# Delta attention, token mixing and two MLPs on one core: the mix's token sum turned, its values split in two

## The chip, the cores and the metric

One core of a Trainium2 chip runs the whole program in a single launch. The metric is the device time in microseconds (us), the median over runs of the same program; smaller is better. The engines are called by their short names: PE (TensorE matmuls, with PEld for its weight loads), DVE (VectorE), ACT (ScalarE), POOL (GpSimd) and SP (the queue that issues most DMAs). Each engine works through its own instructions in the order in which they stand in the program, so an instruction that waits holds up all that stand behind it on that engine.

## The reference

Three stages follow each other on arrays of 4 batches, 768 tokens and 8 heads of 48 (384 columns in all):

```python
# 1 attention, token by token, for each batch and head
y[t] = q[t] @ state
state += beta[t] * outer(k_n[t], v[t] - k_n[t] @ state)
# 2 x is y with heads side by side: mix over the tokens, then an MLP
u = x + (x.transpose(0, 2, 1) @ U @ V).transpose(0, 2, 1)   # U: 768 x 32, V: 32 x 768
x = u + relu(u @ w_ch1) @ w_ch2                              # 384 -> 1536 -> 384
# 3 Fourier mixing, normalisation, a second MLP
u = x + real(fft(fft(x, axis=1), axis=2))
x = u + relu(normalised(u) @ w2_ch1) @ w2_ch2
```

The weights and U and V come as 64-bit floats, q, k, v and beta as 32-bit floats.

## The kernel before, in words

**Stages and tiles.** The attention works on 24 units (chunks) of 128 tokens, six to a batch, numbered 0 to 23. What a unit needs from its keys and queries alone is prepared ahead: scales and 16-bit high and low parts (`s_front`), transposed copies by DMA (`s_turn`), the masked products G (`s_prep_a`, line 841) and their split into a high part `GPh` and a low part `GPl` (`s_split`; the low part is mostly a POOL subtraction, recorded at the helper's line 251), and a triangular inverse `Nf` (`s_prep_b`, `s_prep_c`). Then `s_solve` treats the units one after the other, since each needs the state `S` that the one before left: three small products with `Nf`, corrections, an update of the state and, last, the output `vt` (line 1142, ACT).

**The mix.** `mix_chunk` (line 1010) takes each finished unit. It stores `vt` to DRAM (`xnd`), and multiplies it with the 128 rows of U that belong to it: three fp32 matmuls with `vt` as weights and U as 32 moving columns (line 1026), into `ps_hu`, 128 x 96. DVE adds that to the batch's sum `hu` (lines 1030, 1032). When a batch's six units are in, `s_mix` turns the sum with three PE transposes (line 1283), makes a high and a low part of it (`hst`, lines 1286 and 1288), and multiplies those with three row groups of V (`Vst`: high, high and low part) in fp32r matmuls of 384 columns (line 1305), 128 tokens at a time. DVE adds the tokens' own values (line 1307); scales, splits and a transposing DMA give the input `u` of the first MLP.

**The MLPs.** `s_mlp` handles 8 tiles of 384 tokens in 12 steps each, for both MLPs. A step is nine matmuls into `ps_h` (line 1190), a ReLU on ACT that writes `hh` (line 1196), the low part `hl` on DVE (line 1209; in the attention stage at times PE and ACT, lines 1204 and 1206), and nine matmuls into the accumulators (line 1226), one step behind. `ps_h` of the first MLP has a single PSUM buffer. `s_out1` adds the result, stores it to `x1d` and sums squares.

**The Fourier stage.** It reuses memory that the attention gave up. For each batch, `fold` loads rows of `x1d` forward (SP) and mirrored (indirect DMA on POOL) into `xq`, forms sums and differences `pm` (POOL, line 251), and splits them into `fs` (ACT, line 1451; DVE, line 1453); two rounds of matmuls follow (lines 1485 and 1507). The second MLP's weights are loaded and squared at the same time (`weight2_streams`, lines 483 to 496).

**What sets the order.** No hardware scheduler does. While the program is built, the class `Weave` runs a list scheduler over some twenty generators ("streams"): each says what it wants next, on which engines it may run and for how many modelled nanoseconds; the request with the smallest start time plus its stream's bias is emitted. Biases and prices stand in tables at the top of the file (`PR0`, `PR`, `P2`, `PRICE0` and others), one set until batch 0 is mixed, one until the attention ends, one behind it. `UP` is the number of units whose small sums are made on PE instead of DVE, `UE` the number whose `GPl` is made on PE and ACT instead of POOL.

The two places of the old mix that the change rewrites:

```python
for k in range(KD):                                    # mix_chunk, line 1026
    nc.tensor.matmul(ps[:, k, :], xf[:, 128 * k:128 * k + 128], self.UU[:, c, :], start=True, stop=True)
for k in range(KD):                                    # s_mix, line 1283
    nc.tensor.transpose(ps[0:32, 128 * k:128 * k + 128], hu[:, k, :], self.id32)
```

Of the kernel before, what the change touches and what calls it, by code (L numbers as in the profile page):

```python
# [34 lines left out]
AGE0 = -5  # L35
AGE = 16
EPS0 = -1085
FILL = 47
EPS = -309
UP = 13  # L40
UE = 0
# [3 lines left out]
SPARE = 270  # L45
SPW = 120
PR0 = (-337, -112, -95, -78, -360, -173, -425, 225)
PR = (-41, -98, -140, -142, 118, 51, -956, -408)
ME = -78
MX = -401  # L50
MB = -515
MB0 = -564
P2 = (-467, -323, -887, -360, -372, -386, -1140, -392)
MP = 39
HB = -550
WB1 = -575
WB = -15
PRICE0 = {'p': 1.0, 'v': 1.45, 'a': 0.71, 'g': 0.38}
PRICE = {'p': 1.0, 'v': 0.29, 'a': 0.22, 'g': 0.14}
PRICE2 = {'p': 1.0, 'v': 283.18, 'a': 3.3, 'g': 1.14}  # L60
# [137 lines left out]
def _v(n, rate=1):  # L198
    return 67 + n / (0.96 * rate)
# [14 lines left out]
class Builder:  # L214
# [39 lines left out]
    def setup(self):  # L254
# [23 lines left out]
        self.Vst = c.tile([96, S], F32R, name="Vst")  # L278
# [39 lines left out]
    def mix_parts(self):  # L318

        nc = self.nc  # L320
        self.UU = self.cst.tile([128, NC, 32], F32, name="UU")
        n = NC * 32

        def conv_u(raw, done):
# [3 lines left out]
            nc.scalar.activation(out=self.UU, in_=f, func=ACTF.Copy)  # L328
            self.wv.post("U")

        def conv_v(j):
            def conv(raw, done):
                f = yield from self.from_f64(raw[0:96], self.f64_tile()[0:96])
# [406 lines left out]
    def s_turn(self):  # L740

        nc = self.nc
        for u, _ in self.each():
# [4 lines left out]
            KT = un["KT"] = self.ap1.tile([128, 2, H, 128], F16, tag="KT", name="KT", bufs=NK)  # L748
# [261 lines left out]
    def mix_chunk(self, u):  # L1010
# [5 lines left out]
        if c == 0 and b >= 2:  # L1016
            yield ("hst", b - 2)
# [735 lines left out]
```

## Time and profile before

| what | value |
|---|---|
| median of 3 runs | 1037.67 us (1035.9 to 1040.18) |
| the profiled execution | 1041.91 us, its span 1039.8 us |
| PE busy | 913.1 us, 88% of the span |
| DVE busy | 724.9 us, 70% |
| ACT busy | 548.6 us, 53% |
| POOL busy | 352.2 us, 34% |
| mean granted PE clock | 0.939 of full speed |

The span is the time from the first to the last instruction; the profiled execution's own time is 2.1 us longer. It is one execution, 4.2 us above the median of the runs. An engine's busy share is a mean over three stages: the attention of batch 0 (to about 208 us), the other batches' attention woven with the first MLP (to about 577 us), and the rest of the first MLP, the Fourier stage and the second MLP.

### The profile page before, as it was taken

How to read it: one execution, taken by the hardware profiler on the slowest of the kernel's cores; microseconds unless marked ns; L12 is line 12 of the kernel's file. 1: busy time of each engine (PE TensorE's matmuls, PEld its weight loads, DVE VectorE, ACT ScalarE, POOL GpSimd, SP SyncE). 2: the span in 40 equal slices, each digit the busy share in tenths (PEclk: the TensorE clock that was granted, in tenths of full speed). 3: DMA queues.
4: the chain of work that ended last, by engine and by line, in shares of the span. 5: the costliest groups of instructions: out<-in, count | busy, mean ns of one | idle time of the engine just before them, and what ended most of it. 6: DMA issues, size and time to landing. Idle time of an engine off the chain costs nothing. (4 is left out here: it accounts for less than half of the span.)

```text
span 1039.8 us, 25511 instructions
## 1 busy us (share of the span) xinstructions
PE 913.1 (88%) x10282; PEld 622.6 (60%) x10282; DVE 724.9 (70%) x1664; ACT 548.6 (53%) x1358; POOL 352.2 (34%) x330
## 2 busy tenths in 40 slices
PE   3465777589999899999999879999999999999998
PEld 2344665356777666676676546655756665655655
DVE  6898889898898998998765367765735554444532
ACT  5665676767777766667655244447723232222221
POOL 3554244213444323454110360046555532012010
PEclk8575989589999999999999989999999999999999
DMA  6996677316756565543502546522211311202110
GB/s 189 224 219 163 160 183 174 78 39 146 152 133 162 105 151 112 142 109 79 114 25 70 164 105 192 130 87 71 35 54 50 95 28 54 69 24 61 58 34 23
DMA packets 158253, 110.87 MB, mean 107 GB/s; under 512 B 117484, under 2 KB 146424, under 8 KB 158136
## 3 DMA queue, kind: packets, MB, share of 16 engines
q1 hardware_dynamic: 155688, 102.01, 40.6%
q0 software_dynamic: 2448, 7.24, 2.5%
q8 instruction: 80, 1.31, 0.5%
q14 instruction: 37, 0.30, 0.1%
HBM read 55.63 MB, written 14.16 MB: 67 GB/s over the span
## 5 line engine op out<-in xcount | busy, mean ns | idle before, releaser
L1226 PE MATMUL acc<-w2s,hh 128*128 128x384 f16 x1152 | 281.8, 326 | 4.9 <-DVE u L1624 3.1
L1190 PEld LDWEIGHTS <-w1s 128*128 128x128 f16 x1728 | 163.5, 98 | 114.5 <-issue 14.7
L1196 ACT ACTIVATE hh<-ps_h 128x384 f16<-128x384 f32 x192 | 93.7, 488 | 205.6 <-PE ps_h L1190 201.8
L251 POOL TENSOR_TENSOR GPl<-g,GPh 128x512 f16<-128x512 f32 x92 | 116.1, 1262 | 235.1 <-ACT GPh L244 174.2
L1209 DVE SCALAR_TENSOR_TENSOR hl<-ps_h,hh 128x384 f16<-128x384 f32 x147 | 81.6, 555 | 161.6 <-ACT hh L1196 155.8
L1226 PE MATMUL acc<-w2s,hl 128*128 128x384 f16 x576 | 188.1, 327 | 0.2 <-DVE hl L1209 0.2
L1190 PE MATMUL ps_h<-u,w1s 128*128 128x384 f16 x864 | 169.6, 329 | 11.9 <-DVE hl L1209 10.5
L1190 PE MATMUL ps_h<-uh,w1s 128*128 128x384 f16 x864 | 157.9, 327 | 0.0
L1226 PEld LDWEIGHTS <-hh 128*128 128x128 f16 x1152 | 106.2, 98 | 64.8 <-issue 8.0
L902 PEld LDWEIGHTS <-bd 128*128 128x128 f16 x1728 | 71.6, 99 | 45.7 <-issue 18.6
L1226 PEld LDWEIGHTS <-hl 128*128 128x128 f16 x576 | 56.2, 98 | 38.2 <-DVE hl L1209 0.6
L841 DVE TENSOR_TENSOR g<-ps_g,mask 128x512 f32<-128x512 f32 x96 | 65.6, 683 | 12.1 <-PE ps_g L835 11.0
L834 PE MATMUL ps_g<-KT,BT 128*128 128x256 f16 x192 | 54.0, 301 | 10.0 <-ACT t L993 5.0
L244 ACT ACTIVATE GPh<-g 128x512 f16<-128x512 f32 x75 | 47.0, 626 | 28.0 <-DVE g L841 27.3
L251 POOL TENSOR_TENSOR pair<-x1f,pair 128x384 f16<-128x384 f32 x24 | 22.2, 925 | 111.8 <-ACT pair L1594 106.8
L251 POOL TENSOR_TENSOR pm<-xq 97x768 f32<-97x768 f32 (+1 forms) x16 | 29.3, 1850 | 79.5 <-DMA xq<-x1d 72.1
L835 PE MATMUL ps_g<-K,BT 128*128 128x256 f16 x192 | 54.6, 305 | 1.9 <-DMA K<-KT 1.8
L1068 ACT ACTIVATE rh<-res 128x384 f16<-128x384 f32 x63 | 30.5, 484 | 20.0 <-PE res L1055 10.2
L902 PE MATMUL lanes<-R,bd 128*128 128x32 f16 x768 | 34.7, 179 | 4.5 <-ACT R L244 2.9
L882 DVE TENSOR_TENSOR bd<-Xc,mmask 128x1024 f16<-128x1024 f16 x48 | 34.2, 712 | 5.9 <-ACT Xc L936 5.5
L1055 PEld LDWEIGHTS <-GPh 128*128 128x128 f16 x768 | 30.2, 98 | 9.7 <-issue 6.7
L251 POOL TENSOR_TENSOR kb<-kq,rb 128x384 f32<-128x384 f32 x21 | 18.2, 867 | 50.8 <-DVE rb L658 10.9
(270 smaller groups left out, 1866.6 us busy)
## 6 DMA issues: line engine op xcount, KB each, us to landing
wst<-in_moe_w_ch_dram SPq DMA_DIRECT2D x51, 384.0 KB, 3.4
K<-KT SPq DMA_DIRECT2D x46, 256.0 KB, 3.9
kq<-in_k_dram SPq DMA_DIRECT2D x24, 192.0 KB, 3.8
kq<-in_q_dram SPq DMA_DIRECT2D x24, 192.0 KB, 4.2
vt<-in_v_dram SPq DMA_DIRECT2D x24, 192.0 KB, 2.9
xnd<-vt SPq DMA_DIRECT2D x24, 192.0 KB, 3.5
xn<-xnd SPq DMA_DIRECT2D x24, 192.0 KB, 3.0
x1d<-u SPq DMA_DIRECT2D x24, 192.0 KB, 1.9
```

The lines of the kernel that those rows point to most:

```text
L244: self.nc.scalar.activation(out=out, in_=in_, func=ACTF.Copy)
L251: (self.nc.vector if eng == "v" else self.nc.gpsimd).tensor_tensor(out=out, in0=in0, in1=in1, op=op)
L834: nc.tensor.matmul(o, BT[:, h, :], KT[:, :, h, :], start=i == 0, stop=False, skip_group_check=True)
L835: nc.tensor.matmul(o, BT[:, h, :], K2[:, :, h, :], start=False, stop=True, skip_group_check=True)
L841: nc.vector.tensor_tensor(out=g32.rearrange("p i (a t) -> p (i a) t", a=2), in0=ps.rearrange("p i (a t) -> p (i a) t", a=2), in1=self.mask ...
L882: self.nc.vector.tensor_tensor(out=dst.rearrange("p h (j c) -> p h j c", j=n), in0=x, in1=mask[:, None, :, :].to_broadcast(shape), op=ALU. ...
L902: nc.tensor.matmul(ps[:, h, :], lhs[:, h, :], rhs[:, h, :], start=plus is None, stop=plus is None or h == H - 1)
L1068: nc.scalar.activation(out=t, in_=R, func=ACTF.Copy, scale=-1.0 / SC)
L1190: nc.tensor.matmul(ps[:, i, :], w[:, k, fs], u[x][:, k, :], start=(m == 0), stop=(m == 3 * KD - 1))
L1196: nc.scalar.activation(out=hh, in_=ps, func=ACTF.Relu, scale=1.0 if wi else 1.0 - 2.0 ** -11)
L1209: nc.vector.scalar_tensor_tensor(out=hl, in0=ps, scalar=0.0, in1=hh, op0=ALU.max, op1=ALU.subtract)
L1226: nc.tensor.matmul(acc, h[:, ds_], w, start=(f == 0 and j == 0), stop=(f == KF - 1 and j == 2))
```

## The change

The sum over tokens is now formed turned. U is the stationary operand: `UU` holds its high and its low fp32r part, 64 columns, and the unit's values stream past it. The values are split first: ACT writes the high part `yh` of `vt`, POOL or DVE the rest `yl` (also recorded under the name `yh`). Two fp32r matmuls of 384 columns then give `ps_hu` (64 x 384): both parts of U with `yh`, and U's high part with `yl`. DVE adds all 384 columns into `SH`, a single tile that holds the mix's sum in its lower 64 partitions and the attention's state, moved from `S32`, in its upper 64. At a batch's end there is nothing to transpose: ACT and DVE write the four row groups of `hst` from `SH`, and `Vst` has a fourth group. `KT` has five buffers, not six. All numbers that set the order are new, `UP` is 11 for 13 and `UE` 4 for 0.

```diff
-AGE0 = -5
+AGE0 = 6
...
-UP = 13
-UE = 0
+UP = 11
+UE = 4
...
-PR0 = (-337, -112, -95, -78, -360, -173, -425, 225)
+PR0 = (-219, -196, -172, -118, -335, -164, 311, 58)
...
-        self.Vst = c.tile([96, S], F32R, name="Vst")
+        self.Vst = c.tile([128, S], F32R, name="Vst")
+        self.SH = self.keep.tile([128, H, D], F32, name="SH")
...
-        self.UU = self.cst.tile([128, NC, 32], F32, name="UU")
+        self.UU = self.cst.tile([128, NC, 64], F32R, name="UU")
...
-            nc.scalar.activation(out=self.UU, in_=f, func=ACTF.Copy)
+            nc.scalar.activation(out=self.UU[:, :, 0:32], in_=f, func=ACTF.Copy)
+            yield {"w": _v(n)}
+            nc.vector.tensor_tensor(out=self.UU[:, :, 32:64], in0=f, in1=self.UU[:, :, 0:32].bitcast(F32), op=ALU.subtract)
...
-            KT = un["KT"] = self.ap1.tile([128, 2, H, 128], F16, tag="KT", name="KT", bufs=NK)
+            KT = un["KT"] = self.ap1.tile([128, 2, H, 128], F16, tag="KT", name="KT", bufs=NF + 1)
...
-        if c == 0 and b >= 2:
-            yield ("hst", b - 2)
+        if c == 0 and b >= 1:
+            yield ("hst", b - 1)
...
+        yh, yl = (self.ap1.tile([128, DM], F32R, tag=f"y{x}", name="yh", bufs=1) for x in "hl")
+        yield {"a": _a(DM)}
+        nc.scalar.activation(out=yh, in_=xf, func=ACTF.Copy)
+        e = yield {"w": _v(DM), "g": _g(DM)}
+        self.tt(e, yl, xf, yh.bitcast(F32), ALU.subtract)
         t = yield from self.take()
-        ps = self.psu.tile([128, KD, 32], F32, tag="psu", name="ps_hu")
-        yield {"p": 680 if self.wv.warm else 1280}
-        for k in range(KD):
-            nc.tensor.matmul(ps[:, k, :], xf[:, 128 * k:128 * k + 128], self.UU[:, c, :], start=True, stop=True)
-        yield {"v": _v(32 * KD)}
+        ps = self.psu.tile([128, DM], F32, tag="psu", name="ps_hu")
+        yield {"p": 380 if self.wv.warm else 660}
+        nc.tensor.matmul(ps[0:64], self.UU[:, c, :], yh, start=True, stop=False, skip_group_check=True)
+        nc.tensor.matmul(ps[0:32], self.UU[:, c, 0:32], yl, start=False, stop=True, skip_group_check=True)
+        yield {"v": _v(DM)}
+        hu = self.SH[0:64].rearrange("p h d -> p (h d)")
...
-            nc.vector.tensor_tensor(out=self.hu[b], in0=self.hu[b], in1=ps, op=ALU.add)
+            nc.vector.tensor_tensor(out=hu, in0=hu, in1=ps[0:64], op=ALU.add)
...
-                t, ps = yield from self.mix_bank(n, 0)
-                yield {"p": 330}
-                for k in range(KD):
-                    nc.tensor.transpose(ps[0:32, 128 * k:128 * k + 128], hu[:, k, :], self.id32)
...
+                nc.scalar.activation(out=hst[64:128], in_=hu[0:64], func=ACTF.Copy)
...
+                nc.scalar.activation(out=hst[0:32], in_=hu[0:32], func=ACTF.Copy)
...
+                nc.vector.tensor_tensor(out=hst[32:64], in0=hu[0:32], in1=hst[0:32].bitcast(F32), op=ALU.subtract)
```

Since the numbers are new, the whole order moves. Line numbers of the changed kernel are a few higher for the same statements (1142 is 1150, 1196 is 1204, 1451 is 1455). Three places follow.

**ACT around the first MLP's first step.** `hh` is the step's ReLU, `rh`, `U` and `d` are parts of unit 6's solve, `w1s` and `w2s` are splits of the first MLP's weights. Before:

```order
L244 ACTIVATE GPh<-g_3468 128x512
L365 ACTIVATE w2s<-wf_1794,few 128x384
L936 ACTIVATE Xc<-lanes 128x256
L365 ACTIVATE w1s<-wf_2198,few 128x384
L244 ACTIVATE d_3616<-ps_s 128x384
L365 ACTIVATE w1s<-wf_2198,few 128x384
L244 ACTIVATE R<-lanes 128x256
L365 ACTIVATE w1s<-wf_2198,few 128x384
L244 ACTIVATE R<-lanes 128x256
L1196 ACTIVATE hh<-ps_h 128x384
```

With the change:

```order
L244 ACTIVATE t_142<-Zs 32x8x32
L373 ACTIVATE wf_1544<-wf_1544,few 128x384
L368 ACTIVATE w2s<-wf_1544,few 128x384
L996 ACTIVATE t_144<-ps_x 64x512
L244 ACTIVATE Sst<-SH 64x384
L368 ACTIVATE w2s<-wf_1544,few 128x384
L1150 ACTIVATE vt<-ps_s,dn 128x384
L244 ACTIVATE nf_136<-ps_n 64x8x64
L368 ACTIVATE w1s<-wf_1988,few 128x384
L1027 ACTIVATE yh<-vt 128x384
L1204 ACTIVATE hh<-ps_h 128x384
```

Before, the first `hh` stood behind one of unit 6's three `rh`; now it stands behind all three, the unit's output `vt` and its `yh`. Of the 24 weight splits on ACT (lines 365 and 368), 21 stood ahead of the first `hh`, now 13.

**ACT at the end of the attention.** `vt` is unit 23's output, `fs` the first split of the Fourier stage. Before:

```order
L1142 ACTIVATE vt<-ps_s,dn 128x384
L1286 ACTIVATE hst<-ps_u 32x384 x2
L1196 ACTIVATE hh<-ps_h 128x384 x2
L496 ACTIVATE wst,wsq<-wf_11642 128x384
L1196 ACTIVATE hh<-ps_h 128x384 x2
L496 ACTIVATE wst,wsq<-wf_11642 128x384
L1196 ACTIVATE hh<-ps_h 128x384
L1451 ACTIVATE fs<-pm,few 97x4x193
```

With the change; unit 23's `vt` is the row just ahead of the first one here:

```order
L1027 ACTIVATE yh<-vt 128x384
L1321 ACTIVATE xn<-u_11341,few 128x384
L1204 ACTIVATE hh<-ps_h 128x384 x3
L499 ACTIVATE wst,wsq<-wf_11659 128x384
L1204 ACTIVATE hh<-ps_h 128x384
L499 ACTIVATE wst,wsq<-wf_11659 128x384
L1204 ACTIVATE hh<-ps_h 128x384 x3
L499 ACTIVATE wst,wsq<-wf_11659 128x384
L1204 ACTIVATE hh<-ps_h 128x384
L1289 ACTIVATE hst<-SH 64x384
L1291 ACTIVATE hst<-SH 32x384
L1455 ACTIVATE fs<-pm,few 97x4x193
```

Between the last `vt` and the first `fs` stood five `hh`; now there are eight. On DVE, five `hl` stood between the last sum of the mix and the first `fs`, now seven.

**POOL near the end of the attention.** `GPl` is the low part of G, four to a unit; `yh` is the new subtraction `yl`. Before:

```order
L251 TENSOR_TENSOR kb<-kq,rb 128x384
L251 TENSOR_TENSOR kq<-kq,n_r_9661 128x384
L251 TENSOR_TENSOR GPl<-g_9758,GPh 128x512
L251 TENSOR_TENSOR kb_127<-kb,kb_127 128x8x48
L251 TENSOR_TENSOR kq_119<-kq,kq_119 128x8x48
L251 TENSOR_TENSOR GPl<-g_9891,GPh 128x512
L251 TENSOR_TENSOR GPl<-g_9960,GPh 128x512
L251 TENSOR_TENSOR GPl<-g_9999,GPh 128x512
L251 TENSOR_TENSOR GPl<-g_10351,GPh 128x512
L251 TENSOR_TENSOR GPl<-g_10456,GPh 128x512
L251 TENSOR_TENSOR GPl<-g_10525,GPh 128x512
```

With the change:

```order
L251 TENSOR_TENSOR yh<-vt,yh 128x384
L251 TENSOR_TENSOR kb<-kq,rb 128x384
L251 TENSOR_TENSOR kq<-kq,n_r_9744 128x384
L251 TENSOR_TENSOR GPl<-g_9723,GPh 128x512
L251 TENSOR_TENSOR kb_128<-kb,kb_128 128x8x48
L251 TENSOR_TENSOR kq_120<-kq,kq_120 128x8x48
L251 TENSOR_TENSOR GPl<-g_9825,GPh 128x512
L251 TENSOR_TENSOR GPl<-g_9983,GPh 128x512
L251 TENSOR_TENSOR yh<-vt,yh 128x384
L251 TENSOR_TENSOR GPl<-g_10135,GPh 128x512
L251 TENSOR_TENSOR GPl<-g_10242,GPh 128x512
```

POOL had nothing that depended on a solve; now 24 such subtractions stand among the `GPl`. Each stands behind the `GPl` of at least one whole later unit, where there is one. The number of `GPl` on POOL falls from 92 to 77.

## Rows read from the trace of the kernel before

**Rows 1.** The page, section 1: the span.

```profile
span 1039.8 us, 25511 instructions
```

**Rows 2.** Windows: length, five engines' busy time (instructions), PE clock, DMA, GB/s.

```profile
0.00:208.00 208.00, 122.13 (x1970) 93.96 (x1971) 175.27 (x403) 135.97 (x335) 88.51 (x94) 0.74 0.72 174
208.00:577.00 369.00, 350.26 (x5471) 255.20 (x5470) 308.65 (x683) 250.62 (x630) 115.21 (x99) 0.99 0.49 109
577.00:1040.00 463.00, 440.70 (x2843) 273.48 (x2842) 240.98 (x579) 161.99 (x394) 148.44 (x137) 0.99 0.27 74
```

**Rows 3.** Timeline of PE, 268 to 300 us: start, length, what, count.

```profile
274.93 0.36 PE L1055 MATMUL ps_s<-Ul,GPh 128*128 128x48 f16 x8
275.13 0.48 PE L1226 MATMUL acc<-w2s,hh 128*128 128x384 f16 x2
...
281.80 0.85 PE L1026 MATMUL ps_hu<-UU,vt 128*128 128x32 f32 x6
282.49 0.36 PE L1055 MATMUL ps_s<-rh,nf 128*128 128x48 f16 x8
```

**Rows 4.** Timeline of PE, 346 to 349.5 us.

```profile
347.04 0.44 PE L1305 MATMUL ps_u<-hst,Vst 96*128 96x384 f32 x1 [1.37 <-DVE g L841]
347.32 0.37 PE L902 MATMUL lanes<-Nc,bd 128*128 128x32 f16 x8
```

**Rows 5.** Timeline of PE, 463 to 466.5 us.

```profile
465.86 0.50 PE L1283 MATMUL ps_u<-id,hu 128*32 128x128 f32 x3 [1.00 <-DVE g L841]
```

**Rows 6.** By line and form: count | busy us, mean ns | idle before.

```profile
L251 POOL TENSOR_TENSOR GPl<-g,GPh 128x512 f16<-128x512 f32 x92 | 116.1, 1262 | 235.1 <-ACT GPh L244 174.2 <-DVE GPh L246 25.5 <-PE ps_hu L1026 11.6
...
L251 POOL TENSOR_TENSOR pair<-x1f,pair 128x384 f16<-128x384 f32 x24 | 22.2, 925 | 111.8 <-ACT pair L1594 106.8 <-ACT a L1491 5.0
...
L1142 ACT ACTIVATE vt<-ps_s,dn 128x384 f32<-128x384 f32 x24 | 13.8, 576 | 9.8 <-PE ps_s L1055 9.6
...
L1307 DVE TENSOR_TENSOR u<-ps_u,xn 128x384 f32<-128x384 f32 x24 | 13.3, 556 | 5.9 <-PE ps_u L1305 5.7
...
L1594 ACT ACTIVATE pair<-x1f 128x384 f16<-128x384 f32 x24 | 12.5, 521 | 17.5 <-DVE x1f L1591 17.5
...
L1032 DVE TENSOR_TENSOR hu<-hu,ps_hu 128x96 f32<-128x96 f32 x20 | 5.0, 248 | 7.6 <-PE ps_hu L1026 7.5
```

**Rows 7.** Timeline of ACT, 570 to 606 us [idle before <-releaser].

```profile
574.21 0.58 ACT L1142 ACTIVATE vt<-ps_s,dn 128x384 f32<-128x384 f32 x1 [0.52 <-PE ps_s L1055]
...
591.04 0.49 ACT L1196 ACTIVATE hh<-ps_h 128x384 f16<-128x384 f32 x1 [1.99 <-PE ps_h L1190]
600.49 0.94 ACT L1451 ACTIVATE fs<-pm,few 97x772 f16<-97x772 f32 x1 [8.96 <-POOL pm L251]
```

**Rows 8.** Timeline of POOL, 560 to 625 us.

```profile
577.40 1.37 POOL L1405 MEMSET xq<- 1x1536 f32 x1 [50.28 <-PE ps_hu L1026]
...
592.50 3.71 POOL L251 TENSOR_TENSOR pm<-xq 97x768 f32<-97x768 f32 x2 [6.71 <-DMA xq<-x1d]
```

**Rows 9.** Waits of PE, 577 to 1040 us: total, times, longest.

```profile
PE ps_h L1190 <- DVE hl L1209: 9.5, 3, 8.1
```

**Rows 10.** Chain that ended last: start us, us, what.

```profile
603.48 3.04 PE ps_h L1190 x9
606.51 1.93 PE acc L1226 x9
608.44 1.46 PE ps_h L1190 x9
```

**Rows 11.** Timeline of DVE, 20 to 60 us.

```profile
29.61 1.63 DVE L882 TENSOR_TENSOR bd<-GPh,mmask 128x1024 f16<-128x1024 f16 x1
...
39.42 0.69 DVE L882 TENSOR_TENSOR bd<-Xc,mmask 128x1024 f16<-128x1024 f16 x1
```

**Rows 12.** Timeline of POOL, 28 to 41 us.

```profile
29.23 1.47 POOL L251 TENSOR_TENSOR GPl<-g,GPh 128x512 f16<-128x512 f32 x1
...
37.95 0.91 POOL L251 TENSOR_TENSOR kq<-kq,kq 128x384 f16<-128x384 f32 x1
```

More of the change, by code (lines that the diff above doesn't have):

```diff
@@ L44 @@
 UA = 8
-SPARE = 270
-SPW = 120
-PR0 = (-337, -112, -95, -78, -360, -173, -425, 225)
[L48 to L60, printed above, removed]
+SPARE = 288
+SPW = 98
+PR0 = (-219, -196, -172, -118, -335, -164, 311, 58)
+PR = (-150, -119, -395, -76, 118, -67, -532, -601)
+ME = -102
+MX = -503
+MB = -536
+MB0 = -501
+P2 = (-481, -124, -812, -369, -388, -404, -1582, -255)
+MP = 1
+HB = -662
+WB1 = -218
+WB = -4
+PRICE0 = {'p': 1.0, 'v': 1.74, 'a': 0.42, 'g': 0.24}
+PRICE = {'p': 1.0, 'v': 0.44, 'a': 0.51, 'g': 0.2}
+PRICE2 = {'p': 1.0, 'v': 2028.58, 'a': 0.78, 'g': 0.22}
 SC = 16.0
@@ L347, in mix_parts @@
             src = self.words(self.V[:, HALF * j:HALF * j + HALF])
-            parts.append(([(lambda raw, i=i: raw[32 * i:32 * i + 32], src, 273) for i in range(3)], conv_v(j)))
+            parts.append(([(lambda raw, i=i: raw[32 * i:32 * i + 32], src, 273) for i in range(4)], conv_v(j)))
         return parts
@@ L1049, in f16t, with hmm @@
             return self.ap1.tile([128, H, D], F16, tag=tag, name=tag)
-        def hmm(ps, terms, whole=(), m=128, mode="chain", start=True, stop=True):
+        def hmm(ps, terms, whole=(), m=128, mode="chain", start=True, stop=True, at=0):
             yield {"r" if whole else "p": self.pe(len(terms) * H, 48, m)["p"] + self.pe(len(whole), DM)["p"]}, mode
@@ L1054, in hmm @@
                 for h in range(H):
-                    nc.tensor.matmul(ps[0:m, h, :], lf(h), x[:, h, :], start=start and i == 0 and h == 0,
+                    nc.tensor.matmul(ps[at:at + m, h, :], lf(h), x[:, h, :], start=start and i == 0 and h == 0,
                                      stop=stop and not whole and i == len(terms) - 1 and h == H - 1, skip_group_check=ps is R)
@@ L1139, in s_solve @@
                 St = self.ap2.tile([128, H, D], F16, tag="Sst", name="Sst")
-                yield from self.cp(St[0:64], S32, n, "chain")
+                yield from self.cp(St[64:128], S32, n, "chain")
             yield {"a": _a(n, True) + 94}, "side"
@@ L1277, in s_mix @@
                     self.wv.warm = True
[L1278 to L1290 removed]
+                hu = self.SH.rearrange("p h d -> p (h d)")
+                hst = self.keep.tile([128, DM], F32R, tag="hst", name="hst")
+                yield {"a": _a(DM)}
+                nc.scalar.activation(out=hst[64:128], in_=hu[0:64], func=ACTF.Copy)
+                yield {"a": _a(DM)}, "par"
+                nc.scalar.activation(out=hst[0:32], in_=hu[0:32], func=ACTF.Copy)
+                yield {"v": _v(DM)}, "par"
+                nc.vector.tensor_tensor(out=hst[32:64], in0=hu[0:32], in1=hst[0:32].bitcast(F32), op=ALU.subtract)
+                yield "join"
                 self.wv.post("hst", b)
```

32 lines of the change are left out of this document (11 added, 21 removed).

## The prediction

> **What bounds the kernel now.** I read the span first [rows 1], then the busy times in three stretches [rows 2], and after that only places where PE stands still.
>
> The first stretch, 208 us, is the attention of batch 0. PE is busy for 122 us, DVE for 175 (84%). Preparing a unit and solving it pass through many small DVE and ACT steps there; a little PE work more or less is not what ends this stretch.
>
> The second, 369 us, weaves the other 18 units with the first MLP. PE is busy 350 us (95%) at 0.99 of the 2.4 GHz level, DVE 309 (84%), ACT 251, POOL 115. Work taken off PE shortens this stretch, provided that DVE and the chain of solves keep up.
>
> The third, 463 us, is PE too: 441 us busy, 22 idle. More than a third of that idle time is one wait of 8.1 us, of `ps_h` for DVE's `hl` [rows 9]. The reader can follow its cause: POOL starts to clear `xq` at 577.40, when the attention has freed the memory, and reaches the first `pm` at 592.50, after 6.71 us of waiting for rows of `x1d` [rows 8]. ACT has `fs` next in its order, so it stands idle for 8.96 us and starts it at 600.49, and the sixth `hh` stands behind it [rows 7]. `ps_h` has one buffer, so PE stops. Then nine matmuls take 3.04 us and the next nine 1.93, against 1.46 for the same count after that [rows 10]: 2.1 us more, lost to a start at half speed.
>
> **The change, part by part.** The sum is made against the profiled execution, 1041.9 us; the median of the runs is 4.2 us below it, and I take that off at the end. About 0.5%, 5.2 us, is what a measurement of this kernel can tell from no change.
>
> *The mix's matmuls.* Before, a unit's six records start at 281.80 and the next work at 282.49: 0.69 us of PE [rows 3]. Now there are two fp32r matmuls of 384 columns. The nearest row is `ps_u`, of that kind and width, which starts at 347.04 and is followed at 347.32: 0.28 us [rows 4], so 0.56 for two. The gain is 0.13 x 18 units = 2.3 us in the second stretch. Bounds: 0.44 each if the recorded length counted in full (3.4 us lost), 0.16 each if they ran like fp16 (1.46 / 9, [rows 10]; 6.7 us gained). I take 2.3, since type and width are those of `ps_u`. In the first stretch the six units count for nothing: PE idles there for 86 us.
>
> *The transposes.* Three records of 0.50 us a batch go away [rows 5], for three batches in the second stretch: 1.0 to 1.5 us; I take 1.0, since the last record's tail overlaps with what follows.
>
> *Work moved ahead of the first MLP.* By the order, PE now does unit 6's solve ahead of the first `ps_h`. Counted in matmuls behind the first `ps_h`, there are 13 groups of eight small ones fewer (0.20 us each, [rows 3]), 24 single ones for the state (0.03, an estimate between 0.20 / 8 and 0.36 / 8 of those rows), 16 of 256 columns and 4 of 384 (0.11 and 0.16, from 1.46 / 9): 2.6 + 0.7 + 1.8 + 0.6 = 5.7 us. That is a gain only if the first `ps_h` comes no later, which is the next term.
>
> *The first stretch.* Added on DVE: six evacuations of 384 columns for 96, 0.556 for 0.248 [rows 6], 1.8 us, and one split of U, some 0.3. ACT gets 6 x 0.52 for `yh`, and 16 copies of `GPl` at about 0.58 (the row of `vt`, from PSUM, is nearest), 12 us on 136. POOL loses 16 x 1.26 us of `GPl` and gets six subtractions of 0.93 (as `pair`). Against that, 355 DVE instructions now stand ahead of batch 0's low part of `hst`, where 366 stood: 11 x 0.435 (175.27 / 403), 4.8 us less. But the first `hh` now stands behind the whole of unit 6's solve on ACT, and each unit's mix comes 0.52 + 0.93 us later. I take 0, with -5 and +9 (six times 1.45) as ends.
>
> *The new wait.* `ps_hu` used to need `vt` alone. Now it needs `vt`, `yh`, `yl`: 0.58 + 0.52 + 0.93 = 2.0 us from the last output matmul, and perhaps 2.6 with the hand-overs. PE waits in order, so everything behind it waits too: `ps_h`, the next solve. Before, 6.5 us of PE work lay between (275.13 to 281.80, [rows 3]). Counted in the new order with the pitches above, it is 2.2 us for unit 22 (eight small, three of `ps_h`, nine of `acc`) to 5.6, under 2.9 for four of the 18 units. A POOL instruction of 1.26 or an ACT one of 0.6 us in the way would eat into the others. I take 3 us, four waits of 0.5 and a few small ones; the ends are 0 and 10.
>
> *What else is late.* The buffer taken from `KT` costs nothing: unit u's transposes already stand behind unit u-1's copies into `K2`, which need the solve of unit u-5, and that is what the fifth buffer asks for. `SH` as a single tile costs nothing as long as batch b's `hst` is read before batch b+1's first sum, which the order now demands; the next solve, of about 15 us, covers that. The 24 evacuations are 7.4 us of DVE, of which the 18 in the second stretch lie in its 60 us of idle time.
>
> *The stall behind the attention.* Eight `hh` now stand between the last `vt` and `fs`, for five. The five were done 16.8 us after `vt` began (574.21 to 591.04, [rows 7]); three more steps of 2 x 1.46 us bring the eighth to 25.6, and the ninth would be due at 28.5. `fs` could start at 600.49 - 574.21 = 26.3 us, or 27.7 with `yh` and `yl` in front. So the stall goes, and the slow start with it: 8.1 + 2.1 = 10.2 us; I take 10. On DVE the cover grows by two steps only, and if `xq` comes later still, 2 us remain of the gain. What is late next is the second `fs`, behind four more `hh`, as before.
>
> Sum: 1041.9 - 2.3 - 1.0 - 5.7 + 0 + 3 - 10 = 1025.9, and less 4.2 this is 1021.7: **1022 us**.
>
> **The port.** At 29.61 a DVE product takes 1.63 us with a `GPl` beside it on POOL until 30.70; the same shape at 39.42 takes 0.69 [rows 11, 12]. So a POOL subtraction can hold up a DVE instruction until it ends. The Trainium skill, "SBUF — State Buffer", section "Who interferes with whom", states this as a rule: a DVE instruction with two SBUF inputs and a GpSimd one that reads SBUF share a port, and the later of the two blocks fully. The trace agrees, and by that rule the 24 new subtractions speak against the change. It is the third rival below.
>
> **The rivals.**
>
> 1. *The second stretch keeps its length.* DVE (84%) and the chain of solves, not PE, decide; then only the stall's gain is left: 1041.9 + 3 - 10 - 4.2 = 1031. For it: the shares of DVE; against it: PE's 95%. 0.18.
>
> 2. *Slower: the split on PE's path.* Each of the 18 units' `ps_hu` finds `yl` late because POOL is in a `GPl` (1.26) and ACT in another's copy (0.58), 1.8 us together. 18 x 1.8 = 32 in place of 3 gives 1021.7 + 29 = 1051. It decides from about 1 us a unit, where it eats all of the 19 us gained. For it: the cover fell to 2.2 to 5.6 us; against it: POOL is idle for 254 of 369 us. 0.10.
>
> 3. *The port.* In the second stretch 18 subtractions block DVE for their whole length, 17 us, and with 5.5 us of evacuations DVE rises to 331 of 369 us. Half of it on the path of the solves is 8 us: 1030. Against it: POOL loses 15 `GPl` over the kernel, of 1.26 us. 0.08.
>
> 4. *The first stretch gets shorter* by its 5 us and the new wait costs nothing: 1014. 0.13.
>
> 5. *fp32r is no cheaper here:* the two matmuls take 0.44 us each, the mix loses 3.4 in place of gaining 2.3: 1027. 0.05.
>
> **How the numbers follow.** The forecast has 0.46; its own ends (first stretch -5 to +9, wait -3 to +7, stall 0 to +8, matmuls -4.4 to +5.7) rarely meet, so most of it lies between 1012 and 1032. Below 1009 I leave 0.08, above 1040 some 0.11, nearly all of it the second rival: range **1009 to 1040**. Faster by more than 0.5% (under 1032.5): nine tenths of the forecast, half of the first rival, all of the fourth, two thirds of the third, most of the fifth: 0.41 + 0.09 + 0.13 + 0.05 + 0.03 = 0.71. Slower (over 1042.9): the second rival and a little more, 0.11. The rest, 0.18, is no change.
>
> **What would show it.** Right: the longest wait of `ps_h` behind the attention under 2 us, and no run of nine matmuls at half speed after it; two `ps_hu` records of about 0.44 us at a pitch near 0.28; PE busy in the second stretch for 95% or more; the last `vt` some 6 to 10 us earlier. Wrong: PE idle in front of `ps_hu` for more than a few us in all, DVE over 90% there, or the first `hh` later than before by more than 6 us. The forecast falls if the first `fs` still holds up ACT, or if the first `ps_h` is late by what was moved ahead of it.

## The result, and the profile after

The change made the kernel slower by about 1%. It takes 1049.03 us (median of 4 runs, 1048.49 to 1051.83); the kernel before took 1038.75 us beside it (4 runs). The ratio is 1.0102, with a 95% interval of 1.0085 to 1.0118. The forecast was 1022 us, with 1009 to 1040 as its range. One of the executions behind this page, the profiled one of e8, ran in a slow state and lasted 1600 us, so of e8 only the times of its other four are used.

The page's first line, which answers to [rows 1]:

```profile
span 1046.7 us, 25400 instructions
```

The same three windows as in [rows 2] (length, then busy time and instructions of PE, PEld, DVE, ACT, POOL, then PE clock, DMA share, GB/s):

```profile
0.00:208.00 208.00, 134.16 (x2164) 100.28 (x2165) 180.81 (x404) 156.91 (x385) 85.63 (x90) 0.77 0.71 177
208.00:577.00 369.00, 336.00 (x5160) 234.99 (x5161) 313.54 (x667) 255.82 (x632) 137.88 (x122) 1.00 0.47 106
577.00:1040.00 463.00, 441.83 (x2847) 274.18 (x2846) 239.87 (x575) 163.02 (x395) 146.40 (x137) 0.99 0.29 75
```

The second row is the one to read. PE is busy for 14.3 us less than before, in a window of the same length, and the time is not saved: the gaps in which neither PE nor its weight load runs add up to 32.7 us there, before to 18.7. DVE is busy 4.9 us more, ACT 5.2, POOL 22.7. (Here and below, a gap counts in the window in which it ends.)

Three instructions of ACT mark the stretches (timeline of ACT: start, length, what):

```profile
210.24 0.47 ACT L1204 ACTIVATE hh<-ps_h 128x384 f16<-128x384 f32 x1
...
572.35 0.56 ACT L1150 ACTIVATE vt<-ps_s,dn 128x384 f32<-128x384 f32 x1
...
599.22 0.93 ACT L1455 ACTIVATE fs<-pm,few 97x772 f16<-97x772 f32 x1
```

Before, the first of them stood here:

```profile
216.35 0.48 ACT L1196 ACTIVATE hh<-ps_h 128x384 f16<-128x384 f32 x1
```

The first `hh` starts 6.1 us earlier than before, the last `vt` 1.9 us earlier (574.21, [rows 7]). So between them, in the second stretch, the kernel lost 4.2 us, and it also did less: 53 MLP steps stand before the last `vt`, for 55 before the change, by the count of the `hh` records. Two steps are 2 x 2 x 1.46 = 5.8 us of matmuls [rows 10] that were still to be done. From the last `vt` to the end of the span it is 474.4 us for 465.6: 8.8 more, of which 5.8 are those two steps. The three parts, -6.1, +4.2 and +8.8 us, make up the 6.9 by which the spans differ.

How far single executions can be trusted: before, e11 and e16 have the same instructions up to the last `vt`. Their first `hh` starts at 216.35, 215.64 and 213.97 us; from there to the last `vt` they take 357.86, 357.93 and 357.85. In the same way e7 and e9 take 362.85 and 364.21. Behind the last `vt`, e5 and e17 have the instructions of before and take 462.6 and 461.9 us for its 465.6. So the second stretch can be compared to about 1 us, the first to 2 or 3, the third to about 4.

Batch 0's first `fs` no longer waits for anything, against 8.96 us in [rows 7]; the stall at this place is gone. What PE waits for in the third stretch (total, times, longest), against [rows 9]:

```profile
PE ps_h L1198 <- DVE hl L1217: 6.0, 3, 2.6
PE ps_d L1489 <- ACT fs L1455: 3.6, 1, 3.6
PE acc L1234 <- DVE u L1361: 3.5, 5, 1.4
```

One wait of 8.1 us became several of 1 to 4. All gaps between PE's instructions behind 577 us add up to 21.1 us, for 18.5 before. They moved: between the 55th and the 73rd `hh`, where the stall was, they fell from 10.1 to 7.1 us, and between the 97th and the 160th they grew from 4.2 to 9.0. The largest there is a stall of the same kind, at the sixth of the eight `fs` (timelines of ACT and PE):

```profile
787.92 0.94 ACT L1455 ACTIVATE fs<-pm,few 96x772 f16<-96x772 f32 x1 [5.77 <-POOL pm L251]
788.92 0.50 PE L1489 MATMUL ps_d<-ce,fs 96*128 96x193 f16 x2 [3.63 <-ACT fs L1455]
```

Before, PE waited 1.1 us for that `fs`. From 788.5 to 792.2 us, behind the new wait, the granted clock is 0.50, so PE's slow start came back here too.

The mix itself does what the diff says. Timeline of PE around 308 us, against [rows 3]:

```profile
308.33 0.39 PE L1033 MATMUL ps_hu<-yh,UU 128*64 128x384 f32 x1 [0.81 <-DVE g L844]
308.56 0.34 PE L1034 MATMUL ps_hu<-yh,UU 128*32 128x384 f32 x1
308.73 0.50 PE L1234 MATMUL acc<-w2s,hh 128*128 128x384 f16 x2
```

What PE's matmuls for the tile `ps_hu` waited for (us, times); the first two lines lie in the first 208 us, the third in the second stretch:

```profile
  POOL yh L251: 1.8, 3
  ACT yh L1027: 1.4, 1
  DVE g L844: 3.0, 3
```

The two matmuls take 0.23 and 0.17 us, 0.40 together, for 0.69 before. The wait for the split's two instructions is 3.2 us in all, for the units 0, 1 and 3. In the second stretch PE never waits for them; what it waits for there is mostly `g`, which DVE reads out of the PSUM buffer `psu` before `ps_hu` can have it. `psu` is a single buffer that several products share, `ps_u` among them. The longest lines of that kind (total, times, longest) in the second stretch, after:

```profile
PE ps_u L1309 <- DVE g L844: 5.7, 7, 1.6
PE ps_hu L1033 <- DVE g L844: 3.0, 3, 1.5
```

And before:

```profile
PE ps_u L1305 <- DVE g L841: 3.0, 5, 1.4
PE ps_hu L1026 <- DVE g L841: 0.8, 2, 0.5
```

With the shorter ones, PE's waits for `g` are 12.6 us for 6.1 before, so they hold 6.5 of the 14 us by which its gaps grew there.

### The profile page after: what moved, and what is told of

It is laid out like the page before. It is cut to its first block, busy times and chain, and to the rows that moved or that the text cites. A ratio compares the mean times of both kernels' runs of the same rounds, so it can differ in the third digit from the quotient of the medians.

```text
span 1046.7 us, 25400 instructions
## 1 busy us (share of the span) xinstructions
PE 914.7 (87%) x10181; PEld 610.8 (58%) x10181; DVE 736.6 (70%) x1650; ACT 576.0 (55%) x1412; POOL 369.9 (35%) x348
## 5 line engine op out<-in xcount | busy, mean ns | idle before, releaser
L251 POOL TENSOR_TENSOR GPl<-g,GPh 128x512 f16<-128x512 f32 x77 | 98.6, 1280 | 128.2 <-ACT GPh L244 81.8
L251 POOL TENSOR_TENSOR yh<-vt,yh 128x384 fp32r<-128x384 f32 x24 | 24.8, 1034 | 103.2 <-ACT yh L1027 103.2
L844 DVE TENSOR_TENSOR g<-ps_g,mask 128x512 f32<-128x512 f32 x80 | 54.4, 680 | 6.8 <-PE ps_g L838 6.2
L374 POOL TENSOR_TENSOR w1s<-wf,w1s 128x384 f16<-128x384 f32 x19 | 17.9, 942 | 94.1 <-ACT wf L373 86.1
L244 ACT ACTIVATE GPh<-g 128x512 f16<-128x512 f32 x64 | 40.0, 626 | 14.5 <-DVE g L844 14.2
L885 DVE TENSOR_TENSOR bd<-Xc,mmask 128x1024 f16<-128x1024 f16 x48 | 40.2, 838 | 6.6 <-ACT Xc L939 6.2
L1076 ACT ACTIVATE rh<-res 128x384 f16<-128x384 f32 x62 | 30.2, 486 | 16.2 <-PE res L1066 7.8
```

Source lines behind the costliest of these rows:

```text
L244: self.nc.scalar.activation(out=out, in_=in_, func=ACTF.Copy)
L251: (self.nc.vector if eng == "v" else self.nc.gpsimd).tensor_tensor(out=out, in0=in0, in1=in1, op=op)
L844: nc.vector.tensor_tensor(out=g32.rearrange("p i (a t) -> p (i a) t", a=2), in0=ps.rearrange("p i (a t) -> p (i a) t", a=2), in1=self.mask ...
L885: self.nc.vector.tensor_tensor(out=dst.rearrange("p h (j c) -> p h j c", j=n), in0=x, in1=mask[:, None, :, :].to_broadcast(shape), op=ALU. ...
```

## The experiments

"Before" and "after" are the two kernels. The time of before beside them is 1038.9 us for e1 to e4, 1038.3 for e6 to e9, 1039.3 for e5, e11, e12 and e15, and 1038.4 for e16 and e17. "Drawn anew" means that the scheduler made a new order from the numbers given; "kept" means that the order of the named kernel was held on every engine and only the edit differs.

| run | mix | order | median, us | ratio to before, 95% |
|---|---|---|---|---|
| after | new | new | 1049.0 | 1.0085 to 1.0118 |
| e1 | new | drawn anew with the old numbers | 1068.7 | 1.0221 to 1.0305 |
| e2 | old | drawn anew with the new numbers | 1055.2 | 1.0104 to 1.0186 |
| e3 | new, no low part | after's | 1046.8 | 1.0046 to 1.0094 |
| e4 | new, add of 96 columns | after's | 1048.1 | 1.0052 to 1.0107 |
| e6 | new | after's, third stretch by the old numbers | 1047.6 | 1.0070 to 1.0110 |
| e7 | new | before's, kept | 1045.3 | 1.0045 to 1.0093 |
| e8 | old, without transposes | after's, kept | 1048.2 | 1.0074 to 1.0116 |
| e15 | new, no low part | before's, kept | 1042.2 | 1.0014 to 1.0043 |
| e12 | old, `yh` and `yl` unread | before's, kept | 1045.4 | 1.0042 to 1.0086 |
| e5 | old, more DVE work | before's, kept | 1042.3 | 1.0020 to 1.0062 |
| e17 | old, two thirds of its matmuls left out | before's, kept | 1036.5 | 0.9963 to 0.9996 |
| e11 | old | before's, `fs` moved | 1042.6 | 1.0015 to 1.0054 |
| e16 | old | before's, `fs` moved, `pm` on DVE | 1043.2 | 1.0022 to 1.0050 |
| e9 | new | before's up to `fs`, drawn anew behind it | 1081.1 | 1.0376 to 1.0433 |

**Each half of the change by itself (e1, e2).** The new mix with all of the old numbers, and the old mix with all of the new ones. Of the diff of e1 against after (e2 has the same lines the other way round, in before):

```diff
-AGE0 = 6
+AGE0 = -5
-MX = -503
+MX = -401
-PRICE = {'p': 1.0, 'v': 0.44, 'a': 0.51, 'g': 0.2}
+PRICE = {'p': 1.0, 'v': 0.29, 'a': 0.22, 'g': 0.14}
```

> The new mix with all numbers that set the order (UP and UE too) as in the kernel before. Theory 1, DVE sets the length of the attention and the wide evacuation is the new mix's price: 1040 to 1046 us, some 5 us over the kernel before for 24 times 0.3 us on DVE. Theory 2, the wait for the split values holds up PE: 1045 to 1055, since the old numbers leave it no more room. Theory 3, the new numbers are what costs and the mix itself gains its 3 us of PE: 1033 to 1039.

> The old mix with all numbers of the change. Theory 1: 1040 to 1045, the new kernel less what the wide evacuations cost. Theory 2: under 1040. Theory 3: 1046 to 1055.

Measured: 1068.7 us, far beyond what any theory gave, and 1055.2, just above the highest range. The gaps of PE between 208 and 577 us add up to 29.4 and 30.2 us, near after's 32.7, so one half of the change with the other half's numbers is no measure of either: the scheduler draws the whole order anew, and orders differ by more than the mix is worth. e9 (below) shows how far: 1081 us. From here on, the runs keep an order.

**Parts of the new mix in the new order (e3, e4).**

```diff
-        self.tt(e, yl, xf, yh.bitcast(F32), ALU.subtract)
...
-        nc.tensor.matmul(ps[0:32], self.UU[:, c, 0:32], yl, start=False, stop=True, skip_group_check=True)
```

> The changed kernel in its own order, without the low part of the values: no subtraction on POOL and no second matmul, 24 of each; the sum is made of the high part alone. Theory 1: 1047 to 1050, unchanged within 2 us, since DVE does the same work. Theory 2: 1034 to 1044, since ps_hu waits for ACT's copy alone. Theory 3: unchanged.

```diff
-            nc.vector.tensor_tensor(out=hu, in0=hu, in1=ps[0:64], op=ALU.add)
+            nc.vector.tensor_tensor(out=hu[:, 0:96], in0=hu[:, 0:96], in1=ps[0:64, 0:96], op=ALU.add)
```

> The changed kernel in its own order, with DVE adding only 96 of the 384 columns in 20 of the 24 units (the other columns of the sum stay at the first unit's). Theory 1: 1042 to 1046, since 20 times 0.3 us of DVE go, 15 of them in the second stretch. Theories 2 and 3: 1048 to 1050, unchanged.

Measured: 2.3 and 0.9 us below after by the medians, 3.3 and 2.3 by the ratios. In this order neither the low part nor the wider add is the main price; together they leave 5 to 7 of the 10 us.

**Mix and order taken apart (e7, e8).** e7 has the new instructions at the old ones' places in the program; the planner is still told of the old mix, so that nothing else moves on any engine:

```diff
+        nc.scalar.activation(out=yh, in_=xf, func=ACTF.Copy)
+        self.tt("g", yl, xf, yh.bitcast(F32), ALU.subtract)
         t = yield from self.take()
...
         yield {"p": 680 if self.wv.warm else 1280}
-        for k in range(KD):
-            nc.tensor.matmul(ps[:, k, :], xf[:, 128 * k:128 * k + 128], self.UU[:, c, :], start=True, stop=True)
+        nc.tensor.matmul(ps[0:64], self.UU[:, c, :], yh, start=True, stop=False, skip_group_check=True)
+        nc.tensor.matmul(ps[0:32], self.UU[:, c, 0:32], yl, start=False, stop=True, skip_group_check=True)
```

> The new mix put into the order of before, instruction for instruction: yh and yl stand right behind vt, the two matmuls where the six stood, the add of 384 columns where that of 96 stood; the copies for hst from SH where those from ps_u stood; the three transposes of a batch fall away. All else stands as in before on every engine, fs too, with its stall behind the attention. Theory 'order' (what the 18 units lost comes from the order that the new numbers give, and the mix itself is worth what the prediction said, 2 to 4 us): 1033 to 1039, PE idle between 208 and 577 us about 19 us as before. Theory 'mix' (the new instructions cost it in any order): 1044 to 1052, PE idle there above 28 us.

e8 is the reverse, the old matmuls under the planner's steps of the new ones:

```diff
         yield {"a": _a(DM)}
-        nc.scalar.activation(out=yh, in_=xf, func=ACTF.Copy)
...
         yield {"p": 380 if self.wv.warm else 660}
-        nc.tensor.matmul(ps[0:64], self.UU[:, c, :], yh, start=True, stop=False, skip_group_check=True)
-        nc.tensor.matmul(ps[0:32], self.UU[:, c, 0:32], yl, start=False, stop=True, skip_group_check=True)
+        for k in range(KD):
+            nc.tensor.matmul(ps[:, k, :], xf[:, 128 * k:128 * k + 128], self.UU[:, c, :], start=True, stop=True)
```

> The reverse: the order of the changed kernel, with the six fp32 matmuls of 32 columns where the two stood and the add of 96 columns where that of 384 stood; yh, yl and U's second part left out. The sum over the tokens doesn't reach hst, which is made from a cleared SH (that part of the computation is left out, with the transposes it would need). Theory 'order': 1045 to 1051, within 3 us of the changed kernel. Theory 'mix': 1034 to 1040, as before the change.

Measured: +7 us for the new mix in the old order (1.0069), +10 for the new order with the old mix (1.0095). Both theories were half right, and the two don't add up: in the new order the new mix costs about 1 us, in the old one 7. e7 can be laid beside before instruction by instruction. Timeline of ACT and window of e7:

```profile
219.71 0.48 ACT L1203 ACTIVATE hh<-ps_h 128x384 f16<-128x384 f32 x1
...
582.56 0.58 ACT L1149 ACTIVATE vt<-ps_s,dn 128x384 f32<-128x384 f32 x1 [0.52 <-PE ps_s L1062]
```

```profile
208.00:577.00 369.00, 342.98 (x5331) 242.05 (x5329) 318.61 (x685) 259.80 (x650) 131.43 (x116) 0.99 0.48 109
```

The first `hh` is 3.4 us later and the last `vt` 8.4, with the same 55 steps in front of it: the first stretch lost 3.4 us, the second 5.0, although PE has less to do in it; PE's gaps are 25.8 us in the window, between what the two theories gave. The stretch behind the attention is 4.3 us shorter than in before's execution (461.3 us), but e5 and e17 have 462.6 and 461.9 there without the new mix, so this is no gain of the mix.

**What the second stretch waits for (e17, e12, e5, e15).** All four keep the order of before. e17 takes work off PE and nothing else:

```diff
-        for k in range(KD):
-            nc.tensor.matmul(ps[:, k, :], xf[:, 128 * k:128 * k + 128], self.UU[:, c, :], start=True, stop=True)
+        nc.tensor.matmul(ps[:, 0, :], xf[:, 0:128], self.UU[:, c, :], start=True, stop=True)
+        ps = ps[:, 0:1, :].to_broadcast([128, KD, 32])
```

> The kernel of before in its own order, with one of the mix's three products left out of every three (one of 32 columns for three; the add of 96 columns takes the one result three times, so two thirds of the sum over the tokens are left out): 0.46 us less of PE in each of the 24 units, 8.3 us over the 18 units of the second stretch. If PE bounds that stretch (the prediction's reading): 1030 to 1033. If the solves through DVE and ACT do (theory 'solves'): 1036 to 1040.

Timeline of ACT and window of e17:

```profile
214.62 0.48 ACT L1196 ACTIVATE hh<-ps_h 128x384 f16<-128x384 f32 x1
...
573.02 0.58 ACT L1142 ACTIVATE vt<-ps_s,dn 128x384 f32<-128x384 f32 x1 [0.52 <-PE ps_s L1055]
```

```profile
208.00:577.00 369.00, 345.18 (x5391) 247.62 (x5390) 307.46 (x681) 249.84 (x629) 116.44 (x100) 0.99 0.49 108
```

Measured: 1036.5 us, 2.2 less than before (0.4 to 3.8). From the first `hh` to the last `vt` it is 358.4 us, for 357.9 before: less work on PE made this stretch no shorter. The work taken away is 8.3 us by the pitch of the records (two thirds of 0.69 us, 18 times); PE's busy time in the window, in which records overlap, fell by 5.1. Its gaps grew from 18.7 to 23.7 us. One place shows how (timeline of PE in e17; the same place before is in [rows 3], where the next product starts 0.69 us behind the first and waits for nothing):

```profile
279.77 0.41 PE L1025 MATMUL ps_hu<-UU,vt 128*128 128x32 f32 x2
281.37 0.36 PE L1055 MATMUL ps_s<-rh,nf 128*128 128x48 f16 x8 [1.19 <-ACT rh L1068]
```

PE is done sooner and then waits for ACT's `rh`, a part of the solve. So a busy share of 95% did not make PE the bound for this work; PE stands in an order in which the small matmuls of the solves wait for DVE and ACT. That the MLP's matmuls between them only fill is argued from this: taking some of those away was not tried.

The other side, work added that no matmul reads:

```diff
-            KT = un["KT"] = self.ap1.tile([128, 2, H, 128], F16, tag="KT", name="KT", bufs=NK)
+            KT = un["KT"] = self.ap1.tile([128, 2, H, 128], F16, tag="KT", name="KT", bufs=NF + 1)
...
+        yh, yl = (self.ap1.tile([128, DM], F32R, tag=f"y{x}", name="yh", bufs=1) for x in "hl")
+        nc.scalar.activation(out=yh, in_=xf, func=ACTF.Copy)
+        self.tt("g", yl, xf, yh.bitcast(F32), ALU.subtract)
```

> The kernel of before in its own order with its old mix, plus yh on ACT (0.51 us) and yl on POOL (1.05 us) behind each unit's vt, read by nobody, so PE waits for neither. Theory 'solves' (what stands behind vt on ACT and POOL belongs to the next units' solves): 2 to 6 us longer, 1040 to 1045. Prediction's reading (hidden beside PE): 1038 to 1040.

```diff
+        more = self.keep.tile([128, 2, KD, 32], F16, tag="more", name="more", bufs=1)
+        nc.vector.tensor_copy(out=more, in_=ps[:, None].to_broadcast([128, 2, KD, 32]))
```

> The kernel of before in its own order, with one more DVE instruction for each of the 24 units: a copy of 192 columns of ps_hu, some 0.28 us, about what the longer add of the changed kernel adds, read by nobody. If DVE's time lies on the path of the second stretch (theory 'solves'): 3 to 6 us longer, 1041 to 1045. If PE bounds the stretch and DVE has 60 us to spare (the prediction's reading): 0 to 1 us, 1038 to 1040.

Measured: +6.7 us by the ratio for `yh` and `yl` unread (4.4 to 8.9), +4.3 for the DVE copies (2.1 to 6.4), of 0.35 us each. In e12 the first `hh` stands at 219.84, 3.5 us late, and from there to the last `vt` it is 361.0 us, 3.2 more, so each stretch pays about half. e12 also has five `KT` buffers for six, as e7 and e15 have; in its trace the DMAs that fill `KT` wait for `kq` and `GPl` alone, 15.3 us for 13.4 before, so no wait for a freed buffer shows. e5 is less clean: its copy reads `ps_hu` and so holds `psu` for longer, and PE's matmuls wait 1.5 us for it. In e5's one profiled execution the second stretch grew by only 1 us; where the rest of its median lies I can't show.

```diff
-        self.tt("g", yl, xf, yh.bitcast(F32), ALU.subtract)
...
-        nc.tensor.matmul(ps[0:32], self.UU[:, c, 0:32], yl, start=False, stop=True, skip_group_check=True)
```

> The new mix in the order of before, without yl and the matmul that reads it (the sum loses its values' low part). If the 7 us come from PE's waits for yl, most of them in the first stretch (2.7 us of idle time in front of ps_hu put down to it): 1040 to 1042. If they come from what yh, the wider add and a PE that waits on the solves cost: 1043 to 1046.

Measured: 1042.2, 3.1 us below e7, or 4.2 by the ratios. So of the 7 us that the new mix costs in the old order, 3 to 4 come with `yl` (POOL's instruction, PE's wait for it and the second matmul), and some 3 with all the rest, `yh` and the wider add above all.

**The stall behind the attention (e11, e16).** Here the scheduler's choices in before were written down one by one and played back, with the picks of `fs` and what follows in its stream put later. ACT's order in e11 against before:

```diff
-ACTIVATE fs<-pm,few 97x4x193     behind the 60th hh
+ACTIVATE fs<-pm,few 97x4x193     behind the 63rd hh
-ACTIVATE fs<-pm,few 96x4x193     behind the 64th hh
+ACTIVATE fs<-pm,few 96x4x193     behind the 68th hh
```

> The kernel of before, its order instruction for instruction, with one part of the change's order alone: batch 0's first fs (and its low part on DVE) behind the 63rd hh for the 60th, the second behind the 68th for the 64th, with the 11 products that read them; two loads of xq pass one load of weights. If the prediction's stall term is right, 8.1 us of PE's wait and 2.1 of the slow start go: 1027 to 1031. If the wait comes back at the next late thing (the outputs on DVE, ps_f, the first transform): 1034 to 1038.

Measured: 1042.6 us, 3.5 more than before by the ratio (1.6 to 5.6). The 61st `hh` comes 8.2 us earlier than in before (0.6 of it was there ahead of the stall), and the 73rd is 0.9 us late; where the rest of the 3.5 lies, one execution can't show. Timeline of PE in e11, matmuls of `ps_h` with what they waited for:

```profile
595.97 1.62 PE L1281 MATMUL ps_h<-u,w1s 128*128 128x384 f16 x9 [1.37 <-DVE hl L1301]
599.54 1.62 PE L1281 MATMUL ps_h<-u,w1s 128*128 128x384 f16 x9 [0.48 <-DVE hl L1301]
604.15 1.14 PE L1281 MATMUL ps_h<-u,w1s 128*128 128x384 f16 x6 [1.35 <-DVE hl L1301]
...
614.10 3.01 PE L1281 MATMUL ps_h<-u,w1s 128*128 128x384 f16 x9 [3.13 <-DVE hl L1301]
```

Four waits of 6.3 us in all stand where one of 8.15 stood, and behind the longest nine matmuls take 3.01 us for 1.63, as in [rows 10]; the granted clock is 0.52 from 614.1 to 617.1 us and 1.00 after that. Each wait is for `hl`, which stands on DVE behind other work: conversions of weights at 595, `fs` at 604, the scale of the next tokens at 614. That work is the same as in before, but there it met a PE that had already stood still. Some of it is slowed as well: a scale of three elements takes 1.79 us while POOL works on `pm`. Timeline of DVE in e11:

```profile
608.15 1.79 DVE L1338 TENSOR_SCALAR few<-few 128x3 f32<-128x3 f32 x1
609.98 0.92 DVE L1340 TENSOR_SCALAR few<-few 128x3 uint32<-128x3 uint32 x1
```

To see whether POOL is the cause, e16 puts batch 0's `pm` on DVE and keeps the rest of e11's idea:

```diff
-POOL TENSOR_TENSOR pm<-xq, pm<-pm (12)
+DVE  TENSOR_TENSOR pm<-xq, pm<-pm (12), behind the 61st to the 65th hh
-ACTIVATE fs<-pm,few 97x4x193     behind the 60th hh
+ACTIVATE fs<-pm,few 97x4x193     behind the 63rd hh
```

> The kernel of before, its order instruction for instruction, but batch 0's twelve pm on DVE for POOL, placed behind the 61st to the 65th hh, and its two fs behind the 63rd and the 67th hh. If POOL's pm beside DVE (the port) gave back what the moved fs had gained: 1030 to 1036. If DVE's amount of work there did, or the wait for the rows of x1d: 1040 to 1046, as with fs moved alone or worse.

Timeline of DVE in e16:

```profile
609.38 0.16 DVE L1338 TENSOR_SCALAR few<-few 128x3 f32<-128x3 f32 x1
609.57 0.17 DVE L1340 TENSOR_SCALAR few<-few 128x3 uint32<-128x3 uint32 x1
```

Measured: 1043.2 us, no better than e11. The same instructions now take 0.16 and 0.17 us, so POOL did slow them; but PE still waits 8.5 us for `hl` behind 577 us, in six waits of up to 1.8, where before had 9.5 [rows 9]. Now `hl` stands behind the `pm` instead. Two different fillings of the stall's place, and neither keeps its gain; what it would take to keep it was not found.

**The third stretch (e6, e9).**

```diff
-P2 = (-481, -124, -812, -369, -388, -404, -1582, -255)
+P2 = (-467, -323, -887, -360, -372, -386, -1140, -392)
-PRICE2 = {'p': 1.0, 'v': 2028.58, 'a': 0.78, 'g': 0.22}
+PRICE2 = {'p': 1.0, 'v': 283.18, 'a': 3.3, 'g': 1.14}
```

> The changed kernel with the numbers of before for the second MLP's planner (P2 and PRICE2) alone; the order is that of the changed kernel until the attention has ended. If the 10 us that it lost behind the attention come from those numbers: 1036 to 1042. If they come from what the attention left over (two MLP steps more to do) and from any redrawn order alike: 1045 to 1053.

Measured: 1047.6, 1.4 us below after: the old numbers for the third stretch do not bring back what it lost there. They trade one stall for the other. The wait at the sixth `fs` is down to 0.9 us, but batch 0's first `fs` stands as before the change, and PE waits for `hl` again, for up to 5.1 us (timeline of ACT in e6):

```profile
594.91 0.94 ACT L1455 ACTIVATE fs<-pm,few 97x772 f16<-97x772 f32 x1 [6.42 <-POOL pm L251]
```

e9 is e7 with one more condition:

```diff
+            if b == 0 and i == 0:
+                yield ("hh", 0, 62)
             h_, l_ = (t[0:k, y].rearrange("p a b e -> p (a b) e")[:, :, 0:NO] for y in range(2))
```

> As the kernel with the new mix in the order of before, but batch 0's first fs may be placed only behind the 63rd hh (it stood behind the 60th); the order up to there is the same, behind it the scheduler draws it anew. If the stall of 8 us behind the attention is cured and nothing comes in its place: 8 to 10 us below that kernel, 1023 to 1031. If the redrawn third stretch brings waits of its own, as that of the changed kernel did: no more than 3 us below it.

Measured: 1081.1, 36 us above e7. The scheduler redrew what follows, and put a transpose that the second MLP needs late; the waits of PE behind 577 us (total, times, longest):

```profile
PE ps_h L1197 <- DMA uh<-pair: 23.3, 1, 23.3
```

## Why the prediction was wrong

**The step that failed** first is the sentence on which three terms rest: "Work taken off PE shortens this stretch, provided that DVE and the chain of solves keep up." They don't. e17 takes 8.3 us of PE's records away there (5.1 by the busy time) and that stretch gets no shorter; e7 puts the new mix into an unchanged order and the stretch grows by 5.0 us. A busy share of 95% was read as the bound; it was the share of an engine that fills its waits with the MLP's matmuls. After the change it is 91% (336.00 of 369), where the prediction had named 95% or more as a sign of being right. The Trainium skill, "Perfetto Trace Analysis", section "Identifying the Most-Contended Engine", says to optimize the engine with the highest occupancy first, but to judge TensorE by its MFU (the share of peak arithmetic) and the busy share of its weight loads, not by matmul busy time. The weight loads were busy for 69% of this stretch (255.20 of 369 us, [rows 2]) and DVE for 84%, so by that share PE does not come first, and e17 agrees.

*The mix's matmuls* (-2.3): their price was too high, 0.40 us measured for 0.56 predicted, 0.29 a unit saved and 5.2 over 18 units. By e17 and e7, none of it shortened the stretch.

*The transposes* (-1.0) and *the work moved ahead* (-5.7): PE's busy time in the window fell by 14.3 us, but that is not all work saved. Between the first `hh` and the last `vt` it fell by 10.4 (329.97 us for 340.36), of which 5.8 are the two MLP steps left for later; 4.6 remain, about half of the 9.0 that these terms and the matmuls' promise. The gaps grew by 14.0 us in the window, so nothing of it came out.

*The first stretch* (0, from -5 to +9): -6.1, a little beyond the end, by the new order. The same mix in the old order is the other sign, +3.4 (e7), and `yh` and `yl` alone give +3.5 (e12); executions in the old order differ by 2.4 here.

*The new wait* (+3): its size came out by luck. It was worked out for the 18 units of the second stretch, and there PE waits for `yh` and `yl` not once. All 3.2 us of such waits lie in the first stretch, where the term had none. Leaving out the low part gives 2.3 us back in the new order (e3; its first `hh` stands 2.3 us earlier than after's), 3.1 in the old (e15).

*The stall* (-10): this is the second step that failed. The wait went, as predicted, but the gaps of PE behind 577 us add up to 21.1 us for 18.5. "The stall goes, and the slow start with it" left out what the stall had covered, and that a later `fs` can stall the same way, as the sixth now does (3.6 us of PE, with a slow start). With `fs` moved alone (e11) the 8.2 us are given back within 12 steps and the kernel is 3.5 us slower. The sentence that "on DVE the cover grows by two steps only" named the right engine and priced it at nothing.

*What was missing*: what a new instruction on ACT, POOL or DVE costs the solves. It was set at nothing because each engine had idle time (DVE 60 us in the second stretch). `yh` and `yl`, which nobody reads, cost 6.7 us (e12).

**The rivals.** The first (DVE and the solves decide) had the mechanism, with 0.18; it said that the stretch keeps its length, where it grew by 4.2 us with two steps less done, and it kept the stall's gain, which e11 takes away. The second (the split on PE's path) named 1051 us, near the result, but not by its mechanism: the waits for the split are 3.2 us and not 32, and none of them lies in the second stretch. The third (the port) does not show in the second stretch on the product it was read from: `bd` takes 0.81 us there on average, before 0.83.

What remains open is how the 10 us of the new order with the old mix (e8) come about one by one. The waits that grew are many and short: the longest of PE in the second stretch is 1.6 us. Nearly half of the growth there is waits for `g` in the shared buffer `psu`; e4, which frees that buffer sooner behind `ps_hu`, gained 0.9 us (2.3 by the ratio), and a second buffer was not tried. That the order drawn with the new numbers has more waits than before's is shown; which of the numbers does it was not tried.

## What to carry to other kernels

A busy share of 95% on an in-order engine needn't make it the bound where work that can wait and a chain through other engines share the order: take work off it alone, in the same order, before costing such a gain. An engine's idle time doesn't make an added instruction free if the instruction stands in front of the chain's next step in that engine's queue. And a stall is worth its length only if nothing else used it and nothing of its kind waits behind it: ask what the other engines did meanwhile, and move it alone before counting it.

No version that the runs tried, with the whole computation in it, beats the kernel before. Where a scheduler sets the order, keep the order fixed to price an edit: redrawn, it moved the time by 16 to 36 us here (e2 against before, e1 and e9 against e7).

## What the runs showed of the hardware

The two fp32r matmuls of 384 columns went faster with fewer stationary columns: 0.23 us with 64 and 0.17 with 32 (308.33 to 308.56 to 308.73, after), where `ps_u` with 128 takes 0.28 [rows 4]. In e3, with the first of the two alone, 0.23 is the pitch in most units too. The 0.17 is close to the pace of the fp16 matmuls, 1.46 / 9 = 0.16 [rows 10].

A DVE scale of three elements took 1.79 us beside POOL's `pm` (e11) and 0.16 without it (e16). Between two such scales that `pm` slowed stands a reciprocal of the same size, which it didn't (timeline of DVE in e11):

```profile
610.93 0.18 DVE L1342 RECIPROCAL few<-few 128x3 f32<-128x3 f32 x1
611.14 0.70 DVE L1344 TENSOR_SCALAR few<-few 128x3 f32<-128x3 f32 x1
```

The Trainium skill, "SBUF — State Buffer", section "Who interferes with whom", counts `tensor_scalar` among the operations that can take the port pair shared with GpSimd; the trace agrees, 0.70 to 1.79 us for 0.16 or 0.17. It did not decide the time, as e16 shows.
